# Softmax with tokens on partitions, and pooled values times w_in in float32

## The chip, the cores and the metric

The kernel runs on one core of a Trainium2 chip. The metric is the device time of one execution in microseconds; lower is better. A core has a matrix engine (TensorE, PE in the profile, with its weight loads on a row of their own, PEld), a vector engine (VectorE, DVE), an activation engine (ScalarE, ACT), GpSimd (POOL), and SyncE (SP), whose queue issues all the kernel's transfers. TensorE writes to PSUM, eight banks of 512 float32 values in each of 128 partitions.

## The reference

Four batches of 576 tokens and eight heads of 64 values pass through an attention with 32 memory slots, then through two networks. In short:

```python
a = softmax(phi over the tokens)                       # [b, h, 576, 32]
k_m, v_m = a^T k, a^T v                                # pooled, [b, h, 32, 64]
attn = softmax(q k_m^T / sqrt(64) over the 32 slots)   # [b, h, 576, 32]
x = (attn v_m), heads side by side                     # [2304, 512]
h = x @ w_in;  y = leaky(h, 0.01) @ w_out              # 512 -> 2048 -> 512
out = ((y @ w_a) * (y @ w_b)) @ w_out2                 # 512 -> 1536 -> 512
```

All of it is float32. `q` and `k` are drawn 200 times larger than `v`, so the second softmax is sharp.

## The kernel before

The product of two float32 matrices is made as three TensorE products of the type `fp32r`: each operand is split into a high part `hi` (a cast) and a low part `lo` (the rest), and hi x hi, hi x lo and lo x hi are summed in PSUM (`PASSES`). So most operands exist twice, and each split costs a cast and a subtraction on ScalarE, VectorE or GpSimd.

The attention's last product is folded into the first network: `attn (v_m w_in)` instead of `(attn v_m) w_in`. A batch b has two groups g of four heads; 4 heads x 32 slots make the 128 rows of the contraction.

- `kv_part(b, g)` (L537) makes the first softmax, transposes it on TensorE (`ta`, `tz`), pools keys and values (`km`), normalizes (`kvn`) and turns them (`kvt`). `kbd` gets the keys, block-diagonal, in plain float32; `vm_hi` and `vm_lo` get the values, and for batches 0 and 1 GpSimd copies both into padded tiles `vp_hi`, `vp_lo` (L640 to L655).
- `sc_part(b, g, x)` (L669) makes the second softmax for one piece of tokens x (320 or 256 of the 576) and one group. Two float32 products with 64 stationary columns of `kbd` and the piece of `q` moving give scores with slots on partitions, one PSUM tile `sc`. VectorE's stream transpose puts tokens on partitions (L692); maximum, subtraction, exponential, sum and normalization follow (L700 to L710); a second stream transpose turns back (L711) into `at`, which is split into `ahi` and `alo` (L713 to L716).
- `vw(c, bs)` (L721) multiplies the pooled values with chunk c of `w_in` (512 of 2048 columns, four chunks): in chunk 0 by `vw_pair` for batches 0 and 1 and by `vw_unit` for 2 and 3, later by `vw_unit` for two batches at a time. The results leave PSUM as `vwh` and `vwl`, in `vw_unit` in pieces of 64 partitions (L779 to L788).
- `h_unit` (L810) multiplies `ahi`, `alo` with `vwh`, `vwl` for one piece and 128 columns of the chunk; ScalarE applies the leaky unit, and the result is split into `g`. `y_unit` (L853) multiplies `w_out` with `g` of four units. The second network follows from about 400 us on.
- `weight(kind, c, k)` (L466) loads 512 KB of a weight as 64-bit floats, converts it to float32 (L484 to L503) and splits it (L505 to L509).

Nothing is ordered by hand. `Program` (L102) keeps a list of operations with an engine, or a choice of engines, a cost, tiles, and tokens read and written. A planner in the kernel's source (`urgency`, `order`, `run`) works back from the sequence of `h`, `y` and later products to a due time for each operation, and then fills every engine's queue in order of due time, choosing among engines and among free rooms for tiles. `SLACK` moves due times. At run time each engine works its queue strictly in that order. `ROOMS` (L39) names the rooms: 28 slots of 4 KB a partition, three smaller `sm` rooms for softmax tiles, five `t` rooms, and the PSUM banks: three (`x`) for `ta`, `tz`, `km`, `kvt`, `sc` and `vw`, three for `h`, two for `y`. `two(n)` lets the planner choose VectorE or GpSimd, `copy_by(n)` ScalarE or VectorE. PE's order of `vw` and `sc` among `h` and `y` is the planner's.

Of the kernel before, what the change touches and what calls it, by code (L numbers as in the profile page):

```python
# [10 lines left out]
F32 = mybir.dt.float32  # L11
# [26 lines left out]
NSLOT = 28  # L38
# [5 lines left out]
    "sm": [f"m{i}" for i in range(3)],  # L44
# [9 lines left out]
PRE = 4  # L54
SEVEN = 8
# [281 lines left out]
def tile_mem_attention__leaky_mlp__bilinear_mlp(  # L337
# [84 lines left out]
    tile_of(("vm_hi",), "slot", [4, B, 2 * M], F32R)  # L422
    tile_of(("vm_lo",), "slot", [4, B, 2 * M], F32R)
    VM = [("vm_hi",), ("vm_lo",)]


    VP = [("vp_hi",), ("vp_lo",)]
    for k in VP:
        tile_of(k, "slot", [4, 2, 4 * M], F32R)

    def zeros(T):
        for k in VP + VM:
            nc.gpsimd.memset(T[k].bitcast(F32), 0.0)
        for t in kbd:
            nc.gpsimd.memset(t, 0.0)

    op(
        "POOL", 3.5, zeros,
        w=[("vm", b, g) for b in range(B) for g in range(2)] + [("vp", b, g) for b in range(2) for g in range(2)]
        + [("kbd", i, g) for i in range(2) for g in range(2)],  # L440
        tiles=VM + VP,
    )
# [23 lines left out]
    def weight(kind, c, k, after=()):  # L466
# [4 lines left out]
        if kind not in ("wa", "wb"):  # L471
            tile_of(key, "slot", [2, 512], F32R, heir_of=raw)
# [46 lines left out]
        op(Port({"DVE": 0.62, "POOL": 2.45}), 0, add, r=[("l", key)], w=[a], tiles=[cv], ahead=any_time)  # L519
        if kind in ("wa", "wb"):  # L520
            return
# [7 lines left out]
        op(two(512), 0, lo, r=[a, ("hi", key)], w=[key], tiles=[cv, key], ahead=any_time, slack=SLACK[(kind + "0", k // 2) if first else kind])  # L529
# [7 lines left out]
    def kv_part(b, g):  # L537
# [62 lines left out]
        op("PE", 1.5, k_m, r=[(en, 0), (en, 1), *kvt, rest], w=[km], tiles=[en, *kvt, rest, km])  # L600
# [68 lines left out]
    def sc_part(b, g, x):  # L669

        cols = piece(2 * b + x)
        n = cols.stop - cols.start
        NM = n // 32

        q, sc, sm, at = ("q", b, g) if b else ("q", b, g, x), ("sc", b, g, x), ("sm", b, g, x), ("at", b, g, x)
        tile_of(sc, "x", [n])
        tile_of(sm, "sm", [NM, M])
        tile_of(at, "t", [n])
# [3 lines left out]
        tok = ("sm", b, g, x)  # L682

        def s_sc(T):
            for j in range(2):
                nc.tensor.matmul(
                    T[sc][j * 64:(j + 1) * 64, :], kbd[b % 2][:, 2 * g + j, :], T[q][:, j, (cols.start if b else 0):][:, :n],
                    start=True, stop=True,
                )

        op("PE", 0.56, s_sc, r=[q, ("kbd", b % 2, g)], w=[sc], tiles=[q, sc])
        op("DVE", c_dve(n), lambda T: nc.vector.transpose(T[sm].rearrange("p a m -> p (a m)"), T[sc]), r=[sc], w=[tok], tiles=[sc, sm])  # L692
        mx, sr = (stat((k, g, x, NM), NM) for k in ("mx", "sr"))
        kmx, ksr = ("mx", g, x, NM), ("sr", g, x, NM)
        by = two(n)

        def wide(t):
            return t.unsqueeze(2).to_broadcast([P, NM, M])

        op("DVE", c_dve(n), lambda T: nc.vector.tensor_reduce(mx, T[sm], axis=AX.X, op=ALU.max), r=[tok], w=[kmx], tiles=[sm])  # L700
        op(by, 0, lambda T, e: engines[e].tensor_tensor(T[sm], T[sm], wide(mx), op=ALU.subtract), r=[kmx], w=[tok], tiles=[sm])
        op("ACT", c_act(n), lambda T: nc.scalar.activation(T[sm], T[sm], AF.Exp, scale=1.0 / float(D) ** 0.5), w=[tok], tiles=[sm])

        def s_sum(T):
            nc.vector.tensor_reduce(sr, T[sm], axis=AX.X, op=ALU.add)
            nc.vector.tensor_scalar_add(sr, sr, EPS)
            nc.vector.reciprocal(sr, sr)

        op("DVE", c_dve(n) + 0.3, s_sum, r=[tok], w=[ksr], tiles=[sm])
        op(by, 0, lambda T, e: engines[e].tensor_tensor(T[sm], T[sm], wide(sr), op=ALU.mult), r=[ksr], w=[tok], tiles=[sm])  # L710
        op("DVE", c_dve(n), lambda T: nc.vector.transpose(T[at], T[sm].rearrange("p a m -> p (a m)")), r=[tok], w=[at], tiles=[sm, at])  # L711
        kh, kl = ("ahi", b, g, x), ("alo", b, g, x)
        op(copy_by(n), 0, lambda T, e: copy(e, T[ahi][:, g, cols], T[at]), r=[at], w=[kh], tiles=[at, ahi])  # L713
        op(
            two(n), 0,
            lambda T, e: engines[e].tensor_tensor(T[alo][:, g, cols], T[at], T[ahi][:, g, cols].bitcast(F32), op=ALU.subtract),  # L716
            r=[at, kh], w=[kl], tiles=[at, ahi, alo], slack=SLACK["sc", min(b, 2), x],
        )


    def vw(c, bs):  # L721

        n = FC if c else FC // 2
        m = len(bs) * 2 * M
        if len(bs) == 1:
            for x in range(2):
                for g in range(2):
                    vw_pair(bs[0], x, g)
            return
        for x in range(FC // n):  # L730
            for j in range(4):
                vw_unit(c, bs, x, j, n, m)

    def vw_pair(b, x, g):

        n = FC // 2
        o, w = ("vw", 0, b, x, g), ("win", 0, 2 * x + g)
        tile_of(o, "x", [n])
        cols = slice(x * n, (x + 1) * n)
        hk, lk = ("vwh", 0, b), ("vwl", 0, b)  # L740
# [3 lines left out]
        def prod(T):  # L744
            for j in range(2):
                for k, (v, i) in enumerate(((0, 0), (0, 1), (1, 0))):
                    nc.tensor.matmul(
                        T[o], T[VP[v]][:, 2 * g + j, b, :], T[w][:, i, j * n:(j + 1) * n],
                        start=(j == 0 and k == 0), stop=(j == 1 and k == 2),
                    )  # L750

        op("PE", 0.72, prod, r=[w, ("vp", b, g)], w=[o], tiles=[o, w, *VP], ahead=15.0)
# [4 lines left out]
            r=[o, (hk, g, x)], w=[(lk, g, x)], tiles=[o, hk, lk], slack=SLACK["vw", 0, b],  # L757
        )

    def vw_unit(c, bs, x, j, n, m):  # L760
        o, w = ("vw", c, bs[0], x, j), ("win", c, j if c else 2 * x + j // 2)
        tile_of(o, "x", [n])
        cols, wcols = slice(x * n, (x + 1) * n), slice(0, FC) if c else slice(j % 2 * n, (j % 2 + 1) * n)
        to = slice((j % 2) * 64, (j % 2) * 64 + 64)

        def prod(T):
            for k, (v, i) in enumerate(((0, 0), (0, 1), (1, 0))):
                nc.tensor.matmul(  # L768
                    T[o][0:m], T[VM[v]][:, j, bs[0]:bs[0] + len(bs), :].rearrange("p b m -> p (b m)"), T[w][:, i, wcols],
                    start=(k == 0), stop=(k == 2),  # L770
                )
# [660 lines left out]
```

## Time and profile before

| | us |
|---|---|
| time, median of 3 runs | 807.09 |
| lowest, highest | 805.96, 808.41 |
| the profiled execution | 808.57 |
| its span, first to last instruction | 806.8 |
| PE busy in the span | 779.4 |
| DVE, ACT, POOL busy | 644.7, 394.8, 186.2 |

The profile is of one execution, with a record for every instruction: start, duration, engine, line of the source, tiles. A float32 product that is not `fp32r` has two records, each with a weight load of its own on PEld. Busy time of PE counts records that overlap once. An "idle before" names what released the engine. The column PEclk is the share of TensorE's full clock that was granted. The views used below are busy time by stretches, the timeline of one engine, the chain of work that ended last, the records of one tile, and groups of records by line and form.

### The profile page before, as it was taken

To read this page: it belongs to the slowest core of one execution; us is meant where nothing else is said; L and a number is where in the kernel's file an instruction comes from. 1 tells how busy PE (TensorE), PEld (TensorE's weight loads), DVE (VectorE), ACT (ScalarE), POOL (GpSimd) and SP (SyncE) were. 2 spreads that over 40 slices of the span, in tenths; PEclk is the share of its full clock that TensorE was granted. 3 is DMA by queue.
4 is the path that set the end of the run, shared out by engine and by line. 5 is a ranking of instruction groups with operands and counts; after the bars stand their busy time and mean duration, and the time that the engine had idled before them with its cause. 6 is when DMAs were issued, how large, how long until landed. Compare 5 with 4: busy or idle time off the path is not lost.

```text
span 806.8 us, 12569 instructions
## 1 busy us (share of the span) xinstructions
PE 779.4 (97%) x4514; PEld 678.9 (84%) x4514; DVE 644.7 (80%) x1219; ACT 394.8 (49%) x844; POOL 186.2 (23%) x297
## 2 busy tenths in 40 slices
PE   5779999999999999999999999999999999999998
PEld 4458898999999999999888888888888877888886
DVE  6987799888878986797688788988874666798855
ACT  5547677666557554654355644554421245232120
POOL 3453454240103520420001202342300000124100
PEclk9889999999999999999999999999999999999999
DMA  9984200154023611134888786656687887767402
GB/s 314 379 293 150 82 25 0 54 191 150 0 93 117 238 51 53 54 133 153 316 299 286 276 311 209 231 213 206 208 308 270 287 286 241 243 202 258 153 1 104
DMA packets 56557, 149.97 MB, mean 186 GB/s; under 512 B 7216, under 2 KB 22576, under 8 KB 56496
## 3 DMA queue, kind: packets, MB, share of 16 engines
q1 hardware_dynamic: 56496, 149.18, 53.7%
q8 instruction: 35, 0.57, 0.3%
q14 instruction: 26, 0.21, 0.1%
HBM read 103.55 MB, written 45.61 MB: 185 GB/s over the span
## 4 chain that ended last, share of the span: by engine, by line
PE 86%; DMA 9%; DVE 3%; SPq 1%; ACT 1%; issue 1%; ACTq 0%; DVEq 0%
PE y L868 25%; PE abx L1080 14%; PE h L829 12%; PE o L1174 11%; PE abz L1080 7%; PE os L1289 4%; PE aby L1080 4%; PE vw L768 2%; PE b L1134 2%; PE a L1134 2%; DMA raw_wout<-in_w_out_dram 1%; DMA kv<-in_kv_dram 1%; DMA out_dram<-oacc 1%; DMA raw_wb<-in_w_b_dram 1%; DMA k_wf<-cv_wout_-1_5231 1%; DMA q<-in_qT_dram 1%
## 5 line engine op out<-in xcount | busy, mean ns | idle before, releaser
L868 PE MATMUL y<-g,wout 128*128 128x320 f32 (+1 forms) x1152 | 213.2, 338 | 0.0
L868 PEld LDWEIGHTS y<-g,wout 128*128 128x128 f32 x1152 | 186.6, 189 | 16.8 <-issue 1.9
L1080 PE MATMUL abx<-yb_T,wo 128*128 128x512 f32 x432 | 110.4, 391 | 1.5 <-ACT t L1091 1.5
L1080 PEld LDWEIGHTS abx<-yb_T,wo 128*128 128x128 f32 x432 | 80.0, 188 | 18.0 <-ACT t L1091 2.1
L1174 PE MATMUL o<-p,wout 128*128 128x512 f32 x384 | 94.8, 389 | 0.0
L1174 PEld LDWEIGHTS o<-p,wout 128*128 128x128 f32 x384 | 71.9, 188 | 15.3 <-DVE osum L1187 0.4
L1091 ACT COPY t<-abx 128x512 f32<-128x512 f32 x72 | 42.2, 586 | 85.9 <-PE abx L1080 85.8
L829 PE MATMUL h<-ahi,vwh 128*128 128x320 f32 (+1 forms) x256 | 77.3, 302 | 4.0 <-ACT ahi L408 3.5
L794 ACT ACTIVATE g<-h 128x256 fp32r<-128x256 f32 (+1 forms) x128 | 51.8, 412 | 57.7 <-PE h L829 38.4
L829 PE MATMUL h<-alo,vwh 128*128 128x320 f32 (+1 forms) x256 | 76.3, 298 | 0.3 <-POOL alo L391 0.3
L829 PE MATMUL h<-ahi,vwl 128*128 128x320 f32 (+1 forms) x256 | 76.0, 297 | 0.0
L794 ACT ACTIVATE t<-h 128x320 f32<-128x320 f32 (+1 forms) x128 | 52.3, 410 | 16.8 <-PE h L829 16.5
L883 DVE TENSOR_TENSOR acc<-y,acc 128x320 f32<-128x320 f32 (+1 forms) x72 | 39.7, 555 | 22.4 <-PE y L868 21.7
L845 DVE TENSOR_TENSOR g<-t,g 128x320 fp32r<-128x320 f32 (+1 forms) x98 | 47.6, 503 | 8.7 <-ACT t L794 5.9
L829 PEld LDWEIGHTS h<-ahi,vwh 128*128 128x128 f32 x256 | 48.7, 190 | 7.0 <-ACT ahi L408 3.7
L829 PEld LDWEIGHTS h<-alo,vwh 128*128 128x128 f32 x256 | 48.7, 190 | 1.7 <-POOL alo L391 0.9
L829 PEld LDWEIGHTS h<-ahi,vwl 128*128 128x128 f32 x256 | 48.8, 191 | 0.0
L1088 DVE TENSOR_TENSOR t<-abz,t 128x512 f32<-128x512 f32 x48 | 33.0, 687 | 18.2 <-ACT t L1091 10.0
L783 DVE TENSOR_TENSOR vwl<-vw,vwh 64x512 fp32r<-64x512 f32 (+1 forms) x64 | 39.8, 622 | 8.6 <-ACT vwh L408 6.2
L408 ACT CAST vwh<-vw 64x512 fp32r<-64x512 f32 (+2 forms) x62 | 31.1, 502 | 23.6 <-PE vw L768 9.5
L408 ACT CAST p<-t 128x512 fp32r<-128x512 f32 x30 | 18.7, 622 | 45.6 <-DVE t L1112 26.4
L1187 DVE TENSOR_TENSOR oacc<-o,oacc 128x512 f32<-128x512 f32 x40 | 27.4, 686 | 15.1 <-PE o L1174 14.9
(329 smaller groups left out, 1517.1 us busy)
## 6 DMA issues: line engine op xcount, KB each, us to landing
k_wo<-wo SPq DMA_DIRECT2D x32, 512.0 KB, 4.7
wo<-k_wo SPq DMA_DIRECT2D x32, 512.0 KB, 4.7
raw_wout<-in_w_out_dram SPq DMA_DIRECT2D x24, 512.0 KB, 4.5
raw_win<-in_w_in_dram SPq DMA_DIRECT2D x16, 512.0 KB, 5.2
kv<-in_kv_dram SPq DMA_DIRECT2D x16, 512.0 KB, 10.4
k_yb_T<-yb_T SPq DMA_DIRECT2D x8, 512.0 KB, 7.9
raw_wa<-in_w_a_dram SPq DMA_DIRECT2D x8, 512.0 KB, 4.9
raw_wb<-in_w_b_dram SPq DMA_DIRECT2D x8, 512.0 KB, 5.6
```

What stands on the lines that cost most here:

```text
L408: nc.scalar.copy(dst, src)
L783: nc.vector.tensor_tensor(T[lk][to, j // 2, cols], T[o][i * 64:(i + 1) * 64, :], T[hk][to, j // 2, cols].bitcast(F32), op=ALU.subtract)
L794: nc.scalar.activation(dst, src, AF.Prelu, alpha=0.01)
L829: nc.tensor.matmul(T[o], T[w[u]][:, k, fs], T[a[v]][:, k, cols], start=(k == 0 and i == 0), stop=(k == 1 and i == 2))
L845: lambda T, e: engines[e].tensor_tensor(T[g][:, i, 1, to], T[t], T[g][:, i, 0, to].bitcast(F32), op=ALU.subtract),
L868: nc.tensor.matmul(T[o], w[:, u, es], T[g][:, j, v, :], start=(f == 0 and p == 0), stop=(f == 3 and p == 2))
L883: "DVE", c_dve(m), lambda T: nc.vector.tensor_tensor(T[acc][:, i, :], T[o], T[acc][:, i, :], op=ALU.add),
L1080: nc.tensor.matmul(T[o], T[w][:, which, u, k * P:(k + 1) * P], T[ys[v]][:, k, :], start=first and k == 0 and x == 0, stop=k == 1 and x == ...
L1088: op("DVE", 0.69, lambda T: nc.vector.tensor_tensor(T[to], T[o], T[x], op=ALU.add), r=[o, x], w=[to], tiles=[o, x, to])
L1091: op("ACT", 0.59, lambda T: nc.scalar.copy(T[t], T[X]), r=[X], w=[t], tiles=[X, t])
L1134: nc.tensor.matmul(T[o], T[w][:, k // 2, u, k % 2 * P:(k % 2 + 1) * P], T[ys[v]][:, k, :], start=(k == 0 and x == 0), stop=(k == 3 and x = ...
L1174: nc.tensor.matmul(T[o], T[w][:, u, es], T[g][:, at, v, :], start=(x == 0 and k == 0), stop=(x == 1 and k == 2))
```

## The change

The second softmax is made with tokens on partitions from the start: a piece of `q` is the stationary operand (128 tokens at a time, or three times 107 for a 320-token piece) and `kbd` moves, 64 columns. Both groups of a piece are worked in one `sc_part(b, x)`. Maximum and subtraction read PSUM on VectorE; the result is turned back by TensorE transposes into PSUM (`at`), from which `ahi` and `alo` are taken. Score tiles and `at` take `x` banks; the softmax tile moves from the `sm` rooms into a slot, and there are 29 slots.

The pooled values stay in one float32 tile `vm`, and `w_in` is not split. Each unit of `vw` is two plain float32 products of 64 output rows, one for each j, into the two halves of one PSUM tile, for one batch. Results leave PSUM in pieces of 128 partitions. The padded tiles and the low part of the values are gone. Three planner costs change with it. Cut to its core:

```diff
-NSLOT = 28
+NSLOT = 29
-    "sm": [f"m{i}" for i in range(3)],
+SC, TURN = 0.11, 0.11
...
-        op("PE", 1.5, k_m, r=[(en, 0), (en, 1), *kvt, rest], w=[km], tiles=[en, *kvt, rest, km])
+        op("PE", 0.95, k_m, r=[(en, 0), (en, 1), *kvt, rest], w=[km], tiles=[en, *kvt, rest, km])
...
-        op({"ACT": 0.45, "DVE": 0.5}, 0, ev_hi, r=[o], w=[("vmh", b, g)], tiles=[o, VM[0]])
-        op("DVE", 0.5, ev_lo, r=[o, ("vmh", b, g)], w=[("vm", b, g)], tiles=[o, *VM])
-        if b < 2:
-            op("POOL", 0.5, pad_hi, r=[("vmh", b, g)], w=[("vp", b, g)], tiles=[VM[0], VP[0]])
-            op("POOL", 0.5, pad_lo, r=[("vm", b, g)], w=[("vp", b, g)], tiles=[VM[1], VP[1]])
+        op({"ACT": 0.45, "DVE": 0.5}, 0, ev_v, r=[o], w=[("vm", b, g)], tiles=[o, VM])
...
-    def sc_part(b, g, x):
+    def sc_part(b, x):
+        r, starts = (P, (0, P)) if n == 256 else (107, (0, 107, n - 107))
+        k = len(starts)
+        banks = [(0, 1)] if n == 256 else [(0,), (1,)]
...
+            tile_of(sc, "x", [k, len(gs), P], parts=r)
+            def s_sc(T, gs=gs, sc=sc, qs=qs):
+                for y, at in enumerate(starts):
+                    at += cols.start if b else 0
+                    for z, g in enumerate(gs):
+                        for j in range(2):
+                            nc.tensor.matmul(
+                                T[sc][:, y, z, j * 64:(j + 1) * 64], T[qs[z]][:, j, at:at + r], kbd[b % 2][:, 2 * g + j, :],
+                                start=True, stop=True,
+                            )
...
+            op("PE", SC * len(gs) * k * 2, s_sc, r=[*qs, *(("kbd", b % 2, g) for g in gs)], w=[sc], tiles=[sc, *qs])
+            op("DVE", c_dve(w), top, r=[sc], w=[(kmx, i)], tiles=[sc])
+            op("DVE", c_dve(w), less, r=[sc, (kmx, i)], w=[toks[i]], tiles=[sc, sm])
...
+        for gs, at in zip(banks, ats):
+            tile_of(at, "x", [len(gs), n])
+            def turn(T, gs=gs, at=at):
+                for z, g in enumerate(gs):
+                    for y, c in enumerate(starts):
+                        nc.tensor.transpose(T[at][:, z, c:c + r], T[sm][0:r, y, g, :], ident[0:r, 0:r])
+            op("PE", TURN * len(gs) * k, turn, r=toks, w=[at], tiles=[sm, at])
+            op(copy_by(w, True), 0, lambda T, e, at=at, to=to: copy(e, to(T, ahi), T[at]), r=[at], w=kh, tiles=[at, ahi])
...
+    def vw_unit(c, b, x, g, n):
         def prod(T):
             for j in range(2):
-                for k, (v, i) in enumerate(((0, 0), (0, 1), (1, 0))):
-                    nc.tensor.matmul(
-                        T[o], T[VP[v]][:, 2 * g + j, b, :], T[w][:, i, j * n:(j + 1) * n],
-                        start=(j == 0 and k == 0), stop=(j == 1 and k == 2),
-                    )
+                w = T[ws[j if c else 0]][:, 0, (0 if c else j * n):][:, :n].bitcast(F32)
+                nc.tensor.matmul(T[o][j * 64:(j + 1) * 64, :], T[VM][:, 2 * g + j, b, :], w, start=True, stop=True)
...
+            "PE", 0.03 + 4 * n / 2.4e3, prod, r=[("a", (k[1:])) for k in ws] + [("vm", b, g)], w=[o], tiles=[o, VM, *ws],
...
-        for bs in ([0], [1], [2, 3]) if c == 0 else ([0, 1], [2, 3]):
-            vw(c, bs)
+        for b in range(B):
+            vw(c, b)
```

## Rows read from the trace of the kernel before

**Rows 1.** Busy time by stretches: stretch, length, engines with records, PEclk, DMA share, GB/s.

```profile
31.20:38.00 6.80, 5.44 (x58) 3.63 (x62) 6.80 (x12) 2.09 (x6) 2.94 (x3) 0.50 1.05 344
38.00:48.20 10.20, 6.37 (x70) 4.29 (x62) 10.02 (x25) 6.41 (x18) 6.43 (x15) 1.00 1.03 351
48.20:55.00 6.80, 6.02 (x21) 3.96 (x22) 6.29 (x19) 1.76 (x5) 2.08 (x3) 0.50 0.78 313
60.00:115.00 55.00, 54.43 (x486) 46.65 (x485) 45.00 (x128) 39.58 (x112) 21.55 (x29) 1.00 0.31 96
115.00:400.00 285.00, 284.47 (x1756) 266.35 (x1755) 236.35 (x440) 166.27 (x379) 69.96 (x107) 1.00 0.32 109
```

**Rows 2.** TensorE's timeline, 28 to 50 us: start, length, operation, [idle before].

```profile
32.22 0.63 PE L829 MATMUL h<-ahi,vwh 128*128 128x320 f32 x1 [3.48 <-ACT ahi L408]
...
43.97 0.31 PE L829 MATMUL h<-ahi,vwl 128*128 128x320 f32 x1
...
48.98 1.12 PE L686 MATMUL sc<-q,kbd 128*64 128x256 f32 x4 [4.12 <-DVE sm L692]
```

**Rows 3.** The chain of work that ended last: start, length, work.

```profile
50.10 3.50 PE y L868 x12
...
59.56 0.72 PE vw L747 x6
...
101.24 1.76 PE y L868 x12
...
134.81 2.04 PE vw L768 x9
```

**Rows 4.** Records of the tile `vw`, whole span: duration ns min/median/max, starts, forms.

```profile
L768 PE MATMUL vw<-win,vm_hi x64: 277/389/468, 89.6 to 337.1; 128*128 128x512 f32 x48, 128*128 128x256 f32 x16
...
L747 PE MATMUL vw<-win,vp_hi x32: 277/283/387, 23.2 to 71.4; 128*128 128x256 f32 x32
```

**Rows 5.** TensorE's timeline around `sc`, 75 to 106 us.

```profile
75.39 1.30 PE L686 MATMUL sc<-q,kbd 128*64 128x320 f32 x8 [0.57 <-ACT en L408]
76.61 0.41 PE L829 MATMUL h<-ahi,vwh 128*128 128x320 f32 x1
...
103.19 1.93 PE L868 MATMUL y<-g,wout 128*128 128x320 f32 x12
105.05 0.65 PE L686 MATMUL sc<-q,kbd 128*64 128x256 f32 x4
105.63 0.41 PE L829 MATMUL h<-ahi,vwh 128*128 128x320 f32 x1
105.88 0.30 PE L829 MATMUL h<-alo,vwh 128*128 128x320 f32 x1
```

**Rows 6.** Weight loads of `sc` under way in two short stretches: length, busy (records).

```profile
105.04:105.06 0.02, 0.02 (x2) 1.00 0.00 0
...
105.10:105.12 0.02, 0.02 (x4) 1.00 0.00 0
```

**Rows 7.** TensorE's timeline at the transposes `ta`.

```profile
63.72 1.04 PE L578 MATMUL ta<-ident,phi 128*128 128x128 f32 x8
64.51 2.00 PE L868 MATMUL y<-g,wout 128*128 128x320 f32 x12
```

**Rows 8.** Groups by line and form: busy us, mean ns, idle before.

```profile
L692 DVE STREAM_TRANSPOSE sm<-sc 128x320 f32<-128x320 f32 x8 | 3.7, 490 | 0.1
...
L692 DVE STREAM_TRANSPOSE sm<-sc 128x256 f32<-128x256 f32 x8 | 3.6, 446 | 0.2
...
L636 DVE TENSOR_TENSOR vm_lo<-kvt,vm_hi 64x64 fp32r<-64x64 f32 x16 | 3.5, 222 | 0.4
```

**Rows 9.** VectorE's timeline at the last splits of `w_out`, chunk 0.

```profile
44.27 1.93 DVE L509 TENSOR_TENSOR wout<-cv_wout,wout 128x512 fp32r<-128x512 f32 x3
```

**Rows 10.** GpSimd's timeline ahead of the first `y`.

```profile
43.41 3.02 POOL L643 CAST vp_hi<-vm_hi 64x32 fp32r<-64x32 f32 x8
46.51 2.49 POOL L391 TENSOR_TENSOR g<-t,g 128x320 fp32r<-128x320 f32 x3
```

More of the change, by code (lines that the diff above doesn't have):

```diff
@@ L420, in stat @@
         return small[key]
[L422 to L429, printed above, removed]
+    VM = ("vm",)
+    tile_of(VM, "slot", [4, B, 2 * M])
     def zeros(T):
-        for k in VP + VM:
-            nc.gpsimd.memset(T[k].bitcast(F32), 0.0)
+        nc.gpsimd.memset(T[VM], 0.0)
         for t in kbd:
@@ L437, in tile_mem_attention__leaky_mlp__bilinear_mlp @@
     op(
[L438 to L441, printed above, removed]
+        "POOL", 2.0, zeros, w=[("vm", b, g) for b in range(B) for g in range(2)] + [("kbd", i, g) for i in range(2) for g in range(2)],
+        tiles=[VM],
     )
@@ L470, in weight @@
         tile_of(raw, "slot", [512], I64)
[L471 removed]
+        if kind not in ("wa", "wb", "win"):
             tile_of(key, "slot", [2, 512], F32R, heir_of=raw)
@@ L518, in weight @@
         op(Port({"DVE": 0.68}), 0, join, r=[raw], w=[a], tiles=[raw, cv], ahead=any_time)
-        op(Port({"DVE": 0.62, "POOL": 2.45}), 0, add, r=[("l", key)], w=[a], tiles=[cv], ahead=any_time)
-        if kind in ("wa", "wb"):
+        slack = SLACK[(kind + "0", k // 2) if first else kind]
+        op(Port({"DVE": 0.62, "POOL": 2.45}), 0, add, r=[("l", key)], w=[a], tiles=[cv], ahead=any_time, slack=slack if kind == "win" else 0.0)
+        if kind in ("wa", "wb", "win"):
             return
@@ L528, in weight @@
         op(copy_by(512), 0, hi, r=[a], w=[("hi", key)], tiles=[cv, key], ahead=any_time)
-        op(two(512), 0, lo, r=[a, ("hi", key)], w=[key], tiles=[cv, key], ahead=any_time, slack=SLACK[(kind + "0", k // 2) if first else kind])
+        op(two(512), 0, lo, r=[a, ("hi", key)], w=[key], tiles=[cv, key], ahead=any_time, slack=slack)
     def piece(n):
@@ L667, in q_load @@
             op("DMA", c_dma(P * n * 8), lambda T, q=q, cols=cols: nc.sync.dma_start(T[q], qT[b, g, :, :, cols]), w=[q], tiles=[q], slack=SLACK["q0", x])
-    def sc_part(b, g, x):
+    def sc_part(b, x):
         cols = piece(2 * b + x)
         n = cols.stop - cols.start
[L673 to L678, printed above, removed]
+        r, starts = (P, (0, P)) if n == 256 else (107, (0, 107, n - 107))
+        k = len(starts)
+        banks = [(0, 1)] if n == 256 else [(0,), (1,)]
+        scs, ats = ([(name, b, x, i) for i in range(len(banks))] for name in ("sc", "at"))
+        sm = ("sm", b, x)
+        tile_of(sm, "slot", [k, 2, P])
         ahi, alo = ("ahi", b), ("alo", b)
@@ L693, in sc_part @@
[L693 to L702, printed above, removed]
@@ L704, in s_sum @@
-        def s_sum(T):
[L705 to L711, printed above, removed]
@@ new lines, in sc_part, with flat, by_head @@
+        w = 2 * k * P
+        def flat(T):
+            return T[sm][0:r].rearrange("p k g m -> p (k g m)")
+        def by_head(T):
+            return flat(T).rearrange("p (a m) -> p a m", m=M)
+        op("ACT", c_act(w), lambda T: nc.scalar.activation(flat(T), flat(T), AF.Exp, scale=1.0 / float(D) ** 0.5), w=toks, tiles=[sm])
+        def s_sum(T):
+            nc.vector.tensor_reduce(sr[0:r], by_head(T), axis=AX.X, op=ALU.add)
+            nc.vector.tensor_scalar_add(sr[0:r], sr[0:r], EPS)
+            nc.vector.reciprocal(sr[0:r], sr[0:r])
@@ L738, in vw_pair, with vw @@
+    def vw(c, b):
+        n = FC if c else FC // 2
+        for x in range(FC // n):
+            for g in range(2):
+                vw_unit(c, b, x, g, n)
+    def vw_unit(c, b, x, g, n):
+        o = ("vw", c, b, x, g)
         tile_of(o, "x", [n])
+        ws = [("cv", "win", c, 2 * g + j) for j in range(2)] if c else [("cv", "win", 0, 2 * x + g)]
         cols = slice(x * n, (x + 1) * n)
-        hk, lk = ("vwh", 0, b), ("vwl", 0, b)
+        hk, lk = ("vwh", c, b), ("vwl", c, b)
         tile_of(hk, "slot", [2, FC], F32R)
@@ L835, in h_unit @@
             r=[(n_, b, k, x) for n_ in ("ahi", "alo") for k in range(2)] + [
-                (u, j, 0 if c else f // 2) for u in w for j in range(4 if c or b > 1 else 2)
+                (u, j, 0 if c else f // 2) for u in w for j in range(2)
             ],
@@ L1328, in tile_mem_attention__leaky_mlp__bilinear_mlp @@
             for x in range(2):
-                for g in range(2):
-                    sc_part(b - 1, g, x)
+                sc_part(b - 1, x)
     step, waiting = 0, []
```

103 lines of the change are left out of this document (34 added, 69 removed).

## The prediction

> **What bounds the kernel now.** I read the windows by stage first, TensorE's timeline second, and VectorE's and GpSimd's timelines last. From 60 us on TensorE is never without work: 54.43 of 55 us, then 284.47 of 285 us [rows 1]. VectorE has 10 us free in the first of these stretches and 49 us in the second, ScalarE more. So after 60 us whatever the change takes from VectorE, ScalarE or GpSimd pays nothing, and whatever it adds to TensorE is paid in full.
>
> Before 60 us it is the other way. VectorE is busy 10.02 of 10.20 us (38 to 48.2) and TensorE waits: 3.48 us for `ahi`, the first softmax piece, and 4.12 us for a stream transpose that frees a PSUM bank [rows 2]. After each wait the granted clock stands at 0.50, the 1.2 GHz level, for 6.8 us (31.2 to 38 and 48.2 to 55), in which TensorE is busy 5.44 and 6.02 us [rows 1]: half of that, 2.7 and 3.0 us, is lost. The first `y` product, with which the output starts to be summed, comes at 50.1 us in the chain of work that ended last [rows 3].
>
> **Term 1, pooled values times w_in, chunks 1 to 3.** Before: 48 `vm_hi` products of 512 columns [rows 4] and, by the loop of three passes, half as many with `vm_lo`; nine take 2.04 us [rows 3], so 72 take 16.3 us. After: 24 units of two float32 products, 64 output rows each, side by side in the two column halves. The trace has this very form: `sc`, with 64 of 128 columns. One pair of 256 columns takes 0.58 us to the next start, two pairs of 320 take 1.22 us [rows 5]. With a fixed part f and s per column, 0.58 = f + 256 s and 1.22 = f + 640 s: s is 1.67 ns, f is 0.15 us. Leaving such a run costs more: the next `h` product takes 0.25 us to its successor (105.63 to 105.88) where its twelve-fold neighbours take 0.147 (1.76 for 12) [rows 3, 5]. Entering does too: the twelve `y` passes that start at 103.19 should end at 104.95, and `sc` starts at 105.05 [rows 5]. So a run costs 0.15 + 0.10 + 0.10 = 0.35 us beside its columns. A unit of 512 columns is 0.85 us. How many runs? A batch's two units in a chunk have one due time, and three `x` banks hold them, so I take one run per batch and chunk, 12 in all: 24 x 0.85 + 12 x 0.35 = 24.6 us. Term 1 is +8.3 us; with 8 runs it is +6.9, with 24 it is +12.5.
>
> A float32 pair of 256 columns at 1.67 ns each is four array passes at 2.4 GHz; the three products it replaces are three. That is what the Trainium skill, "FP8 and Floating Point Precision", section TensorE Precision Notes, states: true FP32 takes four passes. By that rule alone the units cost 20.4 us and term 1 is +4.1, which would put the forecast near 814 us. The 0.35 us per run is not in it. "TensorEngine Tiling (Array Packing)", section Key Properties, of the Trainium skill says that changing the tiling mode drains TensorE; the gaps before and after `sc` in the trace agree, and they decide.
>
> **Term 2, the same product in chunk 0.** Before, 16 + 32 `hi` products of 256 columns [rows 4] and half as many with the low parts, 72, at 0.72 us for six [rows 3]: 8.6 us. After, 16 units of 0.427 us and, as these are due half by half, some 10 runs (8 to 16): 6.8 + 3.5 = 10.3 us. Three of the four batches come after 60 us: +1.3 us (0.7 to 2.8).
>
> **Term 3, scores.** Now the query is the stationary operand (128 or 107 columns) and `kbd` moves, 64 columns. Every float32 product is two records, each with a load of its own. No row shows a wide float32 load with so short a product behind it. The nearest: of the four loads of `sc` two have started by 105.06 and all four by 105.12, so a 64-column load follows another in about 55 ns [rows 6]; 128 columns scale to 110 ns. The product itself would need 64 x 1.67 / 2 = 53 ns, so the load is the longer. I take 115 ns a record with 128 columns and 98 ns with 107. A batch has 16 records of the first and 24 of the second: 4.2 us. These products use the full width, like the transposes `ta`, behind which `y` starts with no gap [rows 7], so I add no run cost. Before, a batch of four `sc` units takes 0.85 + 1.07 us of columns and two or three runs of 0.35, 2.8 us. Batches 2 and 3 lie after 60 us: +2.8 us. Ends: loads wholly hidden (66 ns a record), -0.4 us; nothing overlapped (190 ns), +9.6 us. The 320-token half of batch 1 runs just after 50 us, when work is queued: 2.4 us and 0.6 of transposes (term 4) against two units of 0.53 + 0.35, 1.8 us: +1.2 us (0 to 2.4).
>
> **Term 4, turning back.** Ten transposes a batch; eight `ta` take 0.79 us to the next start [rows 7], 0.1 us each. Two late batches, with their start: +2.2 us (2.0 to 2.5).
>
> Sum after 50 to 60 us: 8.3 + 1.3 + 2.8 + 1.2 + 2.2 = +15.8 us.
>
> **Term 5, the start.** VectorE loses the stream transposes (0.44 to 0.49 us each, two for every piece) and `vm_lo` (0.22 us, two for every batch half) [rows 8]. It gains work too: the subtraction of the maximum and `alo` are now fixed on VectorE, where the planner could choose GpSimd before, and the 320-token pieces become three columns of 107 tokens, 768 elements in a partition where 640 were. For the first piece I let that cancel; the 256-token pieces save two transposes of 0.45 us in each half, less one such move, about 1 us each. Up to the end of the `w_out` subtractions at 44.27 + 1.93 us [rows 9] VectorE is 2 to 3 us better off. GpSimd loses the padding copies (3.02 us from 43.41) that stood ahead of the three `g` subtractions (46.51 to 49.0), for which the first `y` waits [rows 10]. So the inputs of `y` could be there at 44 us. But TensorE ends the first piece's `h` at 44.1 us [rows 2], and ahead of that stand now about 3 us of extra scores and transposes, some at 1.2 GHz. The first `y` then starts near 47 instead of 50.1: -3 us. With the 4.12 us wait shortened I give back half of the 3.0 us of half clock: together -4.5 us. Ends: 0, if the longer hold of the PSUM banks renews the wait; -11.5, if `y` starts at 44.3 (5.8 us) and neither half-clock stretch returns (2.7 + 3.0).
>
> Costed at nothing: the dropped split of `w_in` and the halved evictions (128 rows at once where 64 were), all on engines with time to spare after 60 us; the extra slot; the weight loads, which are the same bytes in the same order on SP's queue. The new waits are on TensorE: a transpose waits for VectorE's normalization, and behind it in the queue stand `h` and `y`.
>
> Net +15.8 - 4.5 = +11.3 us. The profiled execution took 808.57 us (span 806.8, the rest lies around it), 1.5 us over the median 807.09; 819.9 by the one, 818.4 by the other, which I give.
>
> **Rivals.** (a) *The sum holds*: 812 to 826 us, likeliest 818.4. (b) *PSUM waits return in the full stretch.* A score bank is held through two VectorE passes (maximum, subtraction) where one transpose freed it, and `at` now takes a bank as well; a 320-token piece needs two banks of three for each. For it: such a wait cost 4.12 us and its half clock 3.0 us [rows 1, 2]. Against: VectorE has 10 us free from 60 to 115. One wait for each late batch is +8.2, with the clock up to +14: 827 to 833 us. (c) *Not slower: the start pays for all.* Mechanism: `y` starts as soon as `h` allows, at 44.3, and the clock doesn't fall: -11.5 us. It decides from the point where the late terms are at most 11.5, which needs their low ends together (8 runs, hidden loads: 6.9 + 0.7 - 0.4 + 0 + 2.0 = 9.2): 805 to 809 us. For it: both big waits are VectorE's. Against: TensorE's own extra work ahead of 44 us. (d) *The pairs don't run side by side*, so the change isn't what it says: 24 x 0.85 + 16 x 0.43, +27 us, 845 us. The `sc` rows speak against.
>
> **How the numbers follow.** (a) 0.62, (b) 0.18, (c) 0.16, (d) 0.04. The range drops (d), half of (c) and the top of (b): 808 to 829 us. About 0.3% (2.4 us) is what a measurement here can tell from no change. Of (c) half is faster and half within 0.3%; of (a) 0.02 lies within: faster 0.08, same 0.10, slower 0.82.
>
> **What would show it.** Right: `vw` runs of two float32 units near 2.1 us with their gaps, `sc` records near 0.11 us apart, TensorE still full from 60 to 400 us and this stretch longer by 12 us or more, the first `y` at 46 to 48 us. Wrong: `sc` records at 60 ns; `vw` runs without gaps; first `y` at 44 us with the clock at 2.4 GHz throughout (then c); TensorE waits of 2 us or more on VectorE between 60 and 115 us (then b).

## The result, and the profile after

The changed kernel takes 815.93 us (median of 4 runs, 815.22 to 816.76), the kernel before, run beside it, 807.75: a ratio of 1.0105, with a 95% interval of 1.0084 to 1.0126. It is slower, by about 8.2 us. The forecast was 818.4, in a range of 808 to 829. The profiled execution took 815.76 us, with a span of 814.0, 7.2 us more than before.

The view read first is again the busy time by stretches, here of the changed kernel; the columns are those of [rows 1], and the last line is the stretch from 400 us to the end.

```profile
31.20:38.00 6.80, 5.86 (x30) 5.41 (x30) 6.80 (x14) 3.91 (x10) 2.60 (x4) 0.57 1.02 310
38.00:48.20 10.20, 9.47 (x134) 7.95 (x133) 8.24 (x22) 6.94 (x20) 2.55 (x3) 1.00 1.03 337
48.20:55.00 6.80, 6.80 (x51) 6.14 (x51) 6.41 (x16) 4.28 (x12) 1.48 (x2) 1.00 0.71 282
60.00:115.00 55.00, 55.00 (x509) 47.06 (x507) 34.53 (x81) 31.87 (x80) 5.62 (x8) 1.00 0.37 115
115.00:400.00 285.00, 285.00 (x1737) 250.41 (x1736) 213.01 (x414) 152.50 (x353) 40.69 (x59) 1.00 0.32 108
400.00:814.00 414.00, 409.27 (x2013) 346.87 (x2011) 313.62 (x521) 156.99 (x279) 58.43 (x78) 1.00 0.65 228
```

The last stretch of the kernel before, which [rows 1] doesn't have:

```profile
400.00:807.00 407.00, 399.62 (x1951) 336.86 (x1949) 313.58 (x530) 156.28 (x279) 67.51 (x96) 1.00 0.67 230
```

From 60 to 400 us TensorE is full to the last hundredth, where before 1.1 us of 340 were free [rows 1]. VectorE has lost 10 us of work from 60 to 115 us and 23 us from 115 to 400 (45.00 to 34.53, 236.35 to 213.01), and nothing came of it, as TensorE is the bound there. The second half-clock stretch (48.2 to 55, [rows 1]) is gone, and the first has grown from 6.8 to 10.3 us (below). After 400 us TensorE waits less: up to the end of the span, 7.2 us are free before (406.8 less 399.62) and 4.7 after; 3.9 us of either is the end of the program, behind the last product.

TensorE's timeline of the changed kernel in the start; start, length, operation, [idle before].

```profile
28.35 3.65 PE L664 MATMUL sc<-kbd,q 128*128 128x64 f32 x16 [3.22 <-DVE cv_wout L483]
31.92 1.30 PE L711 MATMUL at<-ident,sm 107*128 107x107 f32 x6
34.17 1.97 PE L570 MATMUL ta<-ident,phi 128*128 128x128 f32 x8 [0.94 <-DVE alo L720]
35.78 0.61 PE L796 MATMUL h<-ahi,vwh 128*128 128x320 f32 x1
...
45.09 3.10 PE L664 MATMUL sc<-kbd,q 128*107 128x64 f32 x28 [0.47 <-POOL g L391]
47.99 2.01 PE L835 MATMUL y<-g,wout 128*128 128x320 f32 x12
```

The waits of 3.48 and 4.12 us [rows 2] have gone from their places, and a 3.22 us wait stands at 28.35. The releaser named there converts `w_out`, which no score reads. The scores at 28.35 are those of the second piece, and its `q` lands just then. SyncE's queue, and the landing times of these two transfers (min, median, max):

```profile
18.16 1.43 SPq L635 DMA_DIRECT2D q<-in_qT_dram  x2
...
DMA to landing us min/median/max: 9.9/10.0/10.1
```

Issued at 18.16, the first of the two is there at 28.2 us: by its time the new wait goes with a transfer, not with VectorE. The first `h` comes at 35.78 (before 32.22), the first `y` at 47.99 (before 50.03 in this view, 50.10 in [rows 3]). Half clock holds from 26.7 to 37.0 us; it begins 1.6 us after TensorE has run out of work at 25.1, while it still waits:

```profile
26.70:37.00 10.30, 7.71 (x35) 7.33 (x36) 10.23 (x21) 5.94 (x12) 4.29 (x8) 0.50 1.03 342
```

TensorE is busy 7.71 us at 1.2 GHz in it, in the two stretches of the kernel before 5.44 and 6.02 us [rows 1]. Half of the difference, 1.9 us, is what the clock gave back.

The same view where the parts of the sum can be read one by one:

```profile
70.21 1.25 PE L664 MATMUL sc<-kbd,q 128*107 128x64 f32 x12
71.27 0.39 PE L796 MATMUL h<-ahi,vwh 128*128 128x320 f32 x1
...
87.52 2.00 PE L664 MATMUL sc<-kbd,q 128*128 128x64 f32 x16
89.33 0.39 PE L796 MATMUL h<-ahi,vwh 128*128 128x320 f32 x1
89.56 0.30 PE L796 MATMUL h<-alo,vwh 128*128 128x320 f32 x1
...
96.77 0.60 PE L711 MATMUL at<-ident,sm 128*128 128x128 f32 x4
97.30 1.08 PE L587 MATMUL km<-kv,en 128*32 128x128 f32 x32
...
128.03 0.28 PE L796 MATMUL h<-ahi,vwl 128*128 128x256 f32 x1
128.24 1.08 PE L744 MATMUL vw<-cv_win,vm 128*64 128x512 f32 x4
129.25 0.41 PE L796 MATMUL h<-ahi,vwh 128*128 128x320 f32 x1
129.50 0.31 PE L796 MATMUL h<-alo,vwh 128*128 128x320 f32 x1
...
171.39 1.94 PE L744 MATMUL vw<-cv_win,vm 128*64 128x512 f32 x8
173.25 0.42 PE L796 MATMUL h<-ahi,vwh 128*128 128x320 f32 x1
```

A run of one `vw` unit takes 1.01 us to the next start (128.24 to 129.25), one of two units 1.86 (171.39 to 173.25): 0.85 us a unit and 0.16 beside it. The `h` pass ahead of the run takes 0.21 us instead of the 0.12 of its neighbours, the one behind it 0.25 instead of 0.147. That is the 0.35 us per run of term 1 to the hundredth. Score records follow each other in 88 ns with 107 stationary columns (12 in 1.06 us) and in 113 ns with 128 (16 in 1.81 us); four transposes take 0.53 us. The `h` pass behind the scores takes 0.23 us instead of 0.147 (89.33 to 89.56), a cost that the forecast put at nothing.

### The profile page after: what moved, and what is told of

It is laid out like the page before. It is cut to its first block, busy times and chain, and to the rows that moved or that the text cites. A ratio compares the mean times of both kernels' runs of the same rounds, so it can differ in the third digit from the quotient of the medians.

```text
span 814.0 us, 12571 instructions
## 1 busy us (share of the span) xinstructions
PE 795.0 (98%) x4666; PEld 682.5 (84%) x4666; DVE 606.5 (75%) x1119; ACT 377.0 (46%) x793; POOL 115.2 (14%) x167
## 4 chain that ended last, share of the span: by engine, by line
PE 95%; DVE 3%; DMA 1%; ACT 0%; SPq 0%; issue 0%; POOL 0%; ACTq 0%
PE y L835 25%; PE abx L1047 16%; PE h L796 13%; PE o L1141 13%; PE abz L1047 8%; PE os L1256 4%; PE aby L1047 4%; PE vw L744 4%; PE b L1101 2%; PE a L1101 2%; PE sc L664 2%; PE km L587 1%; PE ta L570 1%; DMA out_dram<-oacc 1%; DMA raw_win<-in_w_in_dram 0%; PE at L711 0%
## 5 line engine op out<-in xcount | busy, mean ns | idle before, releaser
L761 ACT ACTIVATE g<-h 128x320 fp32r<-128x320 f32 (+1 forms) x128 | 52.5, 410 | 92.9 <-PE h L796 87.9
L796 PE MATMUL h<-ahi,vwh 128*128 128x256 f32 (+1 forms) x256 | 78.9, 308 | 0.0
L796 PE MATMUL h<-ahi,vwl 128*128 128x256 f32 (+1 forms) x256 | 75.8, 296 | 0.0
L796 PE MATMUL h<-alo,vwh 128*128 128x256 f32 (+1 forms) x256 | 75.8, 296 | 0.0
L812 DVE TENSOR_TENSOR g<-t,g 128x320 fp32r<-128x320 f32 (+1 forms) x115 | 54.3, 476 | 25.8 <-ACT t L761 25.1
L1047 PE MATMUL abx<-yb_B,wo 128*128 128x512 f32 x144 | 36.8, 391 | 0.0
L1047 PE MATMUL abz<-yb_B,wo 128*128 128x512 f32 x144 | 36.6, 390 | 0.0
```

What stands on the lines that cost most here:

```text
L761: nc.scalar.activation(dst, src, AF.Prelu, alpha=0.01)
L796: nc.tensor.matmul(T[o], T[w[u]][:, k, fs], T[a[v]][:, k, cols], start=(k == 0 and i == 0), stop=(k == 1 and i == 2))
L812: lambda T, e: engines[e].tensor_tensor(T[g][:, i, 1, to], T[t], T[g][:, i, 0, to].bitcast(F32), op=ALU.subtract),
L1047: nc.tensor.matmul(T[o], T[w][:, which, u, k * P:(k + 1) * P], T[ys[v]][:, k, :], start=first and k == 0 and x == 0, stop=k == 1 and x == ...
```

## The experiments

The kernels below come from one source that holds both forms of both parts, chosen by two lists: `NEWVW` names the chunks in which the product with `w_in` is float32, `NEWSM` the batches whose second softmax has tokens on partitions. With full lists it has the instruction order of the changed kernel, with empty ones that of the kernel before. Every kernel computes the whole reference. Each change of a list makes the planner order everything anew. Where `NEWSM` is empty, the rooms and the planner's cost of `km` (1.5 us, but for e9 and e12) are those of the kernel before, elsewhere those of the changed one (0.95 us, but for e3 and e10); e8 has 0.95 us and the old rooms. The first `y` is from TensorE's timeline of each kernel's profile; ratios are to the kernel before on the same chip.

| kernel | us | ratio | 95% interval | first `y` |
|---|---|---|---|---|
| the kernel before, beside the change | 807.75 | 1 | | 50.03 |
| the change | 815.93 | 1.0105 | 1.0084 to 1.0126 | 47.99 |
| e1_vw_only | 811.87 | 1.0055 | 1.0036 to 1.0074 | 47.14 |
| e2_softmax_only | 816.35 | 1.0120 | 1.0100 to 1.0139 | 59.03 |
| e3_true_costs | 817.43 | 1.0132 | 1.0111 to 1.0153 | 49.16 |
| e4_vw_serial | 837.34 | 1.0377 | 1.0351 to 1.0403 | 50.14 |
| e5_vw_first_chunk | 812.90 | 1.0061 | 1.0038 to 1.0085 | 49.45 |
| e6_vw_later_chunks | 813.80 | 1.0080 | 1.0052 to 1.0107 | 49.99 |
| e7_softmax_wout_first | 814.87 | 1.0086 | 1.0056 to 1.0115 | 58.39 |
| e8_late_softmax_as_before | 809.86 | 1.0035 | 1.0014 to 1.0056 | 51.51 |
| e9_before_replanned | 805.87 | 0.9977 | 0.9956 to 0.9998 | 50.82 |
| e10_after_replanned | 822.37 | 1.0167 | 1.0134 to 1.0200 | 47.97 |
| e11_scores_twice | 825.42 | 1.0206 | 1.0181 to 1.0232 | 49.71 |
| e12_before_replanned_2 | 806.62 | 0.9984 | 0.9969 to 1.0000 | 48.34 |

My theory going in: the late terms are right, and the early gain comes from VectorE's relief by the new softmax. The rivals: the pairs or the loads cost otherwise; the planner's wrong costs lose the time; or the start goes with the order of work and not with the work removed.

### Each part alone

```diff
-NEWVW, NEWSM = (), ()
+NEWVW, NEWSM = (0, 1, 2, 3), ()     # e1
+NEWVW, NEWSM = (), (0, 1, 2, 3)     # e2
```

> Only the second part of the change: pooled values times w_in as float32 products, softmax as before. Theory (TensorE is full from 60 us, so each part pays its own TensorE time, and the gain at the start is the softmax's): chunks 1 to 3 +9 us, chunk 0 +1 to 2 us, 1 to 2 us back at the start because GpSimd's padding copies are gone; the 4 us wait of scores for a stream transpose and the half clock after it stay. 815 to 819 us, 8 to 11 over before. Rival (the gain at the start comes from this part: padding copies, low parts and the split of w_in): the wait at 45 us is gone, 808 to 812 us.

> Only the first part of the change: softmax with tokens on partitions, turned back by TensorE; pooled values times w_in as three products of split operands as before. Theory: scores and transposes of batches 2 and 3 cost +5 us after 60 us, the start gives back 4 to 7 us (wait for the transpose gone, no half clock after 48 us): 805 to 809 us, no difference from before that can be measured. Rival (the start belongs to the other part): 811 to 814 us.

Both theories missed, in opposite directions: e1 lies in its rival's range, e2 above both of its own. The product alone costs 0.55% (about 4.4 us), with the first `y` at 47.14 and no second half-clock stretch. The new softmax alone, which was to keep the early gain, costs 1.2% (9.7 us), and its first `y` is 9 us late. SyncE's and TensorE's timelines of e2:

```profile
12.01 4.04 SPq L567 DMA_DIRECT2D kv<-in_kv_dram  x4
17.00 2.11 SPq L488 DMA_DIRECT2D raw_wout<-in_w_out_dram  x3
...
54.88 3.65 PE L709 MATMUL sc<-kbd,q 128*128 128x64 f32 x16 [4.16 <-DVE vm_lo L655]
59.03 1.41 PE L1002 MATMUL y<-g,wout 128*128 128x320 f32 x4
```

The plan has put the keys and values of batch 1 ahead of `w_out`, which the kernel before issues at 13.27 us and the changed kernel at 11.54. And the 4.16 us wait is for `vm_lo`, a piece of work that only the other half of the change removes. So the gain at the start was not the softmax's by itself.

### Is it the order of the loads?

```diff
-('wout0', 0): 8.13, ('wout0', 1): 8.13
+('wout0', 0): 10.13, ('wout0', 1): 10.13     # on e2
```

> The softmax part alone, with the due time of the first w_out tiles 2 us earlier, which puts their four transfers ahead of the keys and values of batch 1 on SP's queue, as in the kernel before. Theory (that order made the first y of the softmax part late, 59 instead of 50 us): first y at 49 to 52 us, 807 to 811 us. Rival (TensorE's longer scores at the half clock make it late): first y stays at 57 us or later, 814 to 817 us.

With `w_out` loaded ahead again the time falls by some 0.3% of e2's, within the intervals, and the first `y` still comes at 58.39: TensorE's waits now have 5.2 us of `km` on VectorE's `kvn`. The load order was not the cause of the late `y`; both of the rival's numbers came out, and the rival named the half clock. The windows of e2 bear on it:

```profile
20.00:43.80 23.80, 20.28 (x120) 17.29 (x124) 14.99 (x39) 12.08 (x29) 4.33 (x16) 0.50 0.82 296
...
54.10:60.90 6.80, 6.02 (x27) 6.05 (x28) 4.14 (x12) 2.35 (x6) 3.16 (x10) 0.50 0.58 220
```

TensorE is busy 20.28 us of the first stretch at 1.2 GHz. Half of that, 10 us, is as much as the first `y` is late; the kernel before loses 2.7 us in its first such stretch [rows 1]. In e7 half clock holds from 20.9 to 31.1 and from 41.4 to 51.6 us, with TensorE busy 17.6 us. So the clock can account for most of the delay. That it is the cause, and why it stays low so long with the new softmax alone, is not shown.

### The product by chunks

```diff
-NEWVW, NEWSM = (), ()
+NEWVW, NEWSM = (0,), ()             # e5
+NEWVW, NEWSM = (1, 2, 3), ()        # e6
```

> The float32 product in chunk 0 alone; chunks 1 to 3 with split operands, softmax as before. Theory (the run with this part alone gained its start from chunk 0: no padding copies, no split of the first w_in tiles; its price is in chunks 1 to 3): +1 to 2 us of TensorE in chunk 0, 4 to 6 us back at the start: 801 to 805 us, faster than before. Rival (the start of that run was a lucky plan, not the removed work): 806 to 809 us.

> The float32 product in chunks 1 to 3 alone; chunk 0 with padding copies and split, softmax as before. Theory (TensorE is full there, 24 x 0.85 us and 0.35 us a run against 16.3 us): +8.5 to 10 us, nothing back: 815 to 817 us. Rival (the halved evictions and the missing split of 12 weight tiles help in the full stretch too): 811 us or less.

e6 lies between the theories. Its start is that of the kernel before to a tenth (first `y` 49.99; `sc` waits 4.24 us), and the 24 units with their neighbours cost about what term 1 says: start to next start, its `vw` records of chunks 1 to 3 take 22.56 us against 16.54, and the passes of `h` and `y` next to their 13 runs 2.6 us more than their neighbours, +8.6 together. But the waits after 400 us shrank, with no early work changed:

```profile
400.00:811.50 411.50, 407.12 (x1997) 344.40 (x1995) 311.10 (x525) 153.29 (x272) 57.22 (x78) 1.00 0.64 225
```

4.4 us free instead of the 7.2 of the kernel before. e5 takes away work from VectorE and GpSimd at the start and adds little on TensorE, yet it is 0.61% slower, above both ranges: the first `y` is 0.6 us earlier, no more, and a new wait stands late. TensorE's timeline of e5, then its windows there:

```profile
469.80 2.08 PE L1214 MATMUL abx<-yb_T,wo 128*128 128x512 f32 x6 [2.66 <-ACT t L1225]
...
470.80:474.20 3.40, 3.40 (x9) 2.63 (x8) 2.51 (x5) 2.68 (x5) 3.40 (x7) 0.50 0.48 182
```

A wait of 2.66 us, and half clock for 3.4 us of full work behind it: 2.66 + 1.7 = 4.4 us in a stretch whose work e5 doesn't touch, and where the kernel before waits 1.5 us for `abx`. Its whole loss is 4.9, some 3 of it there.

### The late softmax and its loads

```diff
-NEWVW, NEWSM = (0, 1, 2, 3), (0, 1, 2, 3)
+NEWVW, NEWSM = (0, 1, 2, 3), (0, 1)          # e8
```

> The changed kernel with the softmax of batches 2 and 3 as before (stream transposes), batches 0 and 1 with tokens on partitions; 28 slots and three small rooms. Theory (scores and transposes of the late batches cost 2.8 + 2.2 us of a full TensorE): 5 us under the changed kernel, 809 to 812 us. Rival (VectorE's relief is worth as much): 815 us or more.

```diff
-                        for j in range(2):
+                        for j in (0, 1) if b < 2 else (0, 0, 1, 1):      # e11
                             nc.tensor.matmul(T[sc][:, y, z, ...], T[qs[z]][:, j, at:at + r], kbd[...], ...)
```

> The changed kernel in which each score product of batches 2 and 3 is issued twice, the second over the first, all else in the changed kernel's order: 80 more records on TensorE after 60 us (32 with 128 stationary columns, 48 with 107). Theory (a record is as long as the load of its own stationary operand): 32 x 0.113 + 48 x 0.088 = +7.8 us, 823 to 824.5 us. Rival 1 (a load is hidden behind the product before it, and a record costs its 64 columns at 1.67/2 ns, 53 ns): +4.3 us, about 820. Rival 2 (TensorE's time is not what sets the end there): within 2.4 us of 815.9.

e8 takes 0.70% less than the changed kernel, 5.7 us, as expected; terms 3 and 4 say 2.8 + 2.2 = 5.0 for these two batches, and the rows of the two kernels 2.7 + 2.3 (worked out below). e11 repeats products and changes no order: 1.0% more, 8.1 us by the ratios (9.5 by the medians), where 7.8 were expected. TensorE's timeline of e11:

```profile
71.92 2.38 PE L709 MATMUL sc<-kbd,q 128*107 128x64 f32 x24
74.11 0.39 PE L963 MATMUL h<-ahi,vwh 128*128 128x320 f32 x1
...
111.58 8.20 PE L709 MATMUL sc<-kbd,q 128*128 128x64 f32 x80
119.59 0.36 PE L963 MATMUL h<-ahi,vwh 128*128 128x256 f32 x1
```

24 records of 107 take 2.19 us, 91 ns each, though every product now comes twice with the same operands (the second twelve take 1.13 us, 94 ns each: the end of a run gives a little back); all records of `sc` after 60 us take 15.99 us where the changed kernel's take 7.90, so the 80 more cost 0.101 us each. The rival's 53 ns (hidden loads) is out.

### Side by side, and the planner's costs

```diff
-                nc.tensor.matmul(T[o][j * 64:(j + 1) * 64, :], T[VM][:, 2 * g + j, b, :], w, start=True, stop=True)
+                nc.tensor.matmul(T[o], T["vm", b // 2][:, 2 * g + j, b % 2, :], w, start=j == 0, stop=j == 1)   # e4
...
-        op("PE", 0.95, k_m, ...
+        op("PE", 1.45, k_m, ...                                        # e3, and SC 0.11 -> 0.21
-            "PE", 0.03 + 4 * n / 2.4e3, prod, ...
+            "PE", 0.35 + 4 * n / 2.4e3, prod, ...                      # e3
```

> The changed kernel, but the two float32 products of a vw unit are 128 columns wide, with zeros in the half that is not theirs, and are summed one after the other in PSUM instead of running side by side in two column halves. Same result. Theory (side by side halves the time, and entering and leaving the two-column mode costs 0.35 us for each of 26 runs): 24 x 0.85 + 16 x 0.43 = 27 us more, 26 x 0.35 = 9 us less, so +18 us on the changed kernel, 831 to 837 us. Rival (pairs do not run side by side): no more than the changed kernel, 806 to 816 us. If side by side holds but a run costs nothing: 843 us.

> The changed kernel with TensorE's costs in the planner set to what the trace shows: 0.21 us for a score product, 1.45 for km, 0.35 more for every unit of vw. Nothing that is computed changes. Theory (TensorE's work is what costs, whoever plans it): within 2 us of the changed kernel, 814 to 818 us. Rival (the plan is late because it thinks these products half as long): 3 us or more faster, 810 to 813 us.

In e4 the two products are 128 rows wide, with zeros, and follow each other. It takes 2.7% more than the changed kernel, 22 us, just above the range expected. One run of two units, from TensorE's timeline of e4, against the 1.86 us above:

```profile
164.83 1.93 PE L1006 MATMUL y<-g,wout 128*128 128x320 f32 x12
166.59 3.59 PE L915 MATMUL vw<-cv_win,vm 128*128 128x512 f32 x8
169.62 0.68 PE L967 MATMUL h<-ahi,vwh 128*128 128x256 f32 x1
170.14 0.28 PE L967 MATMUL h<-alo,vwh 128*128 128x256 f32 x1
```

The run takes 3.03 us, and the pass behind it 0.52 instead of 0.12: 1.7 us a unit, twice the 0.85. So the halves do run side by side. Over all `vw` runs after 60 us, with the passes next to them, e4 has 17.5 us more than the changed kernel, of the 21.3 us that its span is longer. e3 tells the planner what the rows measure, and is not faster (1.0132 against 1.0105), as expected. It is one order; as the next section shows that another order can move the changed kernel by 5 us, it says only that true costs by themselves don't win the loss back.

### What a new order does by itself

```diff
-        op("PE", 1.5, k_m, ...       # the kernel before
+        op("PE", 1.6, k_m, ...       # e9; 1.3 in e12
...
-        op("PE", 0.95, k_m, ...      # the changed kernel
+        op("PE", 1.0, k_m, ...       # e10
```

> The kernel before with one planner cost changed, that of the pooling product `km` from 1.5 to 1.6 us: the same instructions on the same data, in another order (some 1,086 of 2,603 lines of TensorE's order differ as a list). It sizes what a re-plan alone does, on which the earlier runs leave the start and the waits after 400 us hanging. Theory: a re-plan moves the time by several us, by waits and half clock before 60 us and by waits after 400 us, while the stretch from 60 to 400 us stays full: anything from 804 to 814 us, and away from 807.7 by more than 2.4 us. Rival: re-planning is worth under 2.4 us (805.3 to 810.1), and what was seen before 60 us in the runs belongs to the work removed or added.

> The kernel before with the planner's cost of `km` at 1.3 us instead of 1.5: the same instructions; the orders differ in a tenth as many places as in the other re-planned one (218 lines of TensorE's). Theory (what a re-plan does is large even when it moves little): 804 to 814 us and off from 807.7 by more than 2.4 us. Rival: a small re-ordering does nothing, 805.3 to 810.1 us.

> The changed kernel with the planner's cost of `km` at 1.0 instead of 0.95 us: same instructions, another order. Theory: 812 to 821 us, with the first `y` off from 48.0 by more than 1 us, TensorE full from 60 to 400 us as in the changed kernel, and any difference found before 60 and after 400 us. Rival: within 2.4 us of 815.9, the first `y` within 1 us of 48.0: then the early start of the changed kernel is the work's and not the plan's.

For the kernel before the rival held: 0.23% and 0.16% faster, less than 2.4 us, though waits moved by microseconds. For the changed kernel one small cost moves the time by 0.6%, about 5 us by the ratios and 6.4 by the medians, above both ranges, with the first `y` at the same time as in the changed kernel, as the rival had it. The stretch to 60 us and the one from 400 us, of e12, e9 and e10 in turn:

```profile
0.00:60.00 60.00, 41.21 (x343) 29.89 (x344) 49.61 (x123) 34.93 (x88) 30.87 (x71) 0.83 0.88 304
400.00:805.70 405.70, 398.62 (x1947) 336.05 (x1945) 313.35 (x529) 155.44 (x278) 67.95 (x96) 1.00 0.66 230
...
0.00:60.00 60.00, 39.36 (x330) 29.11 (x331) 48.66 (x120) 33.81 (x82) 28.04 (x66) 0.83 0.93 322
400.00:805.20 405.20, 399.71 (x1958) 337.81 (x1956) 306.65 (x517) 150.31 (x269) 60.22 (x81) 1.00 0.66 228
...
0.00:60.00 60.00, 43.78 (x396) 35.21 (x396) 44.34 (x103) 33.62 (x81) 8.25 (x19) 0.83 0.91 316
400.00:820.30 420.30, 412.84 (x2027) 348.82 (x2025) 314.36 (x528) 153.88 (x275) 70.61 (x99) 1.00 0.65 226
```

After 400 us 7.1, 5.5 and 7.5 us are free, in the changed kernel 4.7 and in the kernel before 7.2. In e10 `at` waits 4.4 us for VectorE at 34.62 and `km` 3.2 us for a load; to 60 us TensorE is busy 43.78 us at a lower clock, in the changed kernel 45.74 at 0.86. So the part of the changed kernel's gain that lies before 60 and after 400 us, some microseconds, is lost again by the next order of the same instructions. And e12, with all the work of the kernel before, has its first `y` at 48.34, while e11, with the changed kernel's very order up to there, has it at 49.71, 1.7 us later than the changed kernel: in single executions that time alone is no sign of relief.

## Why the prediction was right, point by point

The sign was right, and so was its reason: after 60 us TensorE is full, the change adds to it, and VectorE's relief pays nothing there. At 400 us the changed kernel has 9.7 us more work left (409.27 against 399.62 us busy), though at 60 us it was 2.9 us of `h` ahead (rows below): the full stretch cost some 12.5 us, where the forecast asked for 12 or more. The time came out 2.5 us under the forecast. Worked out over the two profiled executions, as start to next start of TensorE's records:

- *Term 1* (+8.3): the price per unit and per run was right (0.85 and 0.35 us; two-unit runs show the same). There are 15 runs in chunks 1 to 3, not 12, so by the same prices +9.2, against the 16.54 us that the old records take. The Trainium skill, "FP8 and Floating Point Precision", section TensorE Precision Notes, counts four passes for true FP32: the 0.85 us of a unit agrees with it, and by it alone the term would be +4.1.
- *Term 2* (+1.3): this was mis-sized. After 60 us, chunk 0's `vw` records take 4.67 us (before 5.48), for 34 of 64 records where before 42 of 72 were still to come, not three quarters. The passes next to their runs take 0.9 us more than their neighbours, so a unit costs 0.66 us, as counted (0.64); but an old one cost 0.59 where I counted 0.54, with edges that I didn't count, 0.2 us of them next to scores. Measured +0.3 us.
- *Term 3* (+2.8 for the late batches): the records I put at 115 and 98 ns take 113 and 88, 7.90 us after 60 us, and the passes behind their four runs 0.3 us more. The old scores took 4.64 us and the passes next to their five runs 0.9 us more, 5.5 in all, where I counted 5.6. Measured +2.7 us. The +1.2 for the early piece stays as counted: its 28 records at 45.09 take 2.90 us.
- *Term 4* (+2.2): 20 transposes of the late batches take 2.0 us, the passes behind them 0.25 more; six of batch 1, which stand in the +1.2, take 0.6 us after 60 us.
- *The sum* of these, 9.2 + 0.3 + 2.7 + 1.2 + 2.3, is 15.7 us; 15.8 was forecast.
- *Term 5* (-4.5): at 60 us the changed kernel has 24 passes of `h` fewer still to come (720 against 744, rows below; at 0.12 us each 2.9 us), but six more transposes, 0.6 us. With the +1.2 taken as counted, that makes term 5 -3.5 us. The first `y` at 48.0 is in the forecast band, the second half-clock stretch is gone, and the clock gave back 1.9 us where 1.5 was forecast. But the reason given, relief of VectorE and GpSimd, is not shown: the softmax alone delays the first `y` by 9 us, float32 in chunk 0 alone moves it 0.6 us, a re-plan with nothing removed 1.7 (e12), and another execution of the same order 1.7 as well (e11). The size was a microsecond off, the mechanism stays open.
- *Not in the sum*: TensorE's waits after 60 us fell by 3.5 us, 1.1 before 400 us and 2.4 after (`os` and `abx`), and the passes at the edges of such waits by another 1.7. I treated what comes after 400 us as fixed. The net of +11.3 was too high by 4.1 us (7.2 of span, 8.2 by the medians), and these waits are more than that; terms 1 to 5 were each off by a microsecond or less. That terms 1 and 2 missed by as much in opposite directions is luck. All of these together, 15.7 - 3.5 - 5.2, are 7.0 of the 7.2 us. That the waits go with the order is shown in part: e6 loses 2.8 us of them after 400 with the softmax untouched, and e9, which removes nothing, 1.7.
- *Rival (b)*: no wait of 2 us on VectorE between 60 and 115 us; the row of that stretch is full. The 4.4 us wait of `at` in e10's start is not for a bank but for VectorE's normalization, the other new wait that the prediction names. *Rival (c)*: the late sum was not at its low end, and the clock did fall. *Rival (d)* fell with e4.

Records of `h` on TensorE after 60 us, in the kernel before and in the changed one: length of the stretch, then busy time and records of PE, PEld and ACT.

```profile
60.00:806.80 746.80, 109.97 (x744) 103.37 (x744) 88.17 (x248) 1.00 0.51 174
...
60.00:814.00 754.00, 111.59 (x720) 101.13 (x720) 85.53 (x240) 1.00 0.50 174
```

## What to carry to other kernels

Read first which stretch is full and on which engine: a change that trades that engine's time for any other's loses there, however much the other sheds. Price an added product by its records in the trace with the edges to its neighbours, and count the runs, as the edges of 15 runs are a fifth of the product's new time here and over half of term 1. Where a planner orders the work, re-plan the unchanged kernel once or twice for the size of that effect before a few microseconds at the start are put down to work removed; here it was under 2 us for one kernel and 5 for the other. Read the granted clock of the start in every run as well: in e2 it weighs as much as the delay that was to be explained.

## What the runs showed of the hardware

- The time of a float32 product of 64 moving columns goes with the columns of its stationary operand: 113 ns a record with 128, 88 to 94 ns with 107, also when every product is issued twice (e11). A load of 64 columns follows another in 55 ns [rows 6], about the same per column, so the load is taken to set the pace; its 64 columns alone, at the 1.67 ns of [rows 5], would be 53 ns.
- A run of 64-row products between 128-row ones costs 0.35 us: 0.09 in the pass ahead, 0.16 in the run, 0.10 in the pass behind. The Trainium skill, "TensorEngine Tiling (Array Packing)", section Key Properties, says that a change of the tiling mode drains TensorE; the rows agree and give the price. The 0.09 ahead goes with the 64 rows: ahead of the 128-row float32 products of e4, twelve `y` passes take 1.76 us (164.83 to 166.59), as undisturbed ones do. Of the 0.10 behind, 0.08 is there behind full-width scores too (89.33).
- One wait of 2.66 us late in e5 was followed, a microsecond after work came back, by 3.4 us at 1.2 GHz with TensorE full: the clock made it a loss of 4.4 us.
